# Attention weights and output gradients copied from SBUF to SBUF in place of a store and a load through DRAM

## The chip, the cores and the metric

One NeuronCore of a Trainium2 chip runs the whole program. The metric is the device time of one execution in microseconds (us). Before the change the median of three executions was 715.21 us (713.69 to 716.18). TensorE multiplies matrices, VectorE and ScalarE do the elementwise work, GpSimd (POOL in the profile) and SyncE (SP) issue most transfers (304 and 234 of the 567 issues in the trace of the kernel before). The order of each engine's instructions comes with the build: the two profiles of one program (bwd_only and bwd_only_again) have the rows of SyncE and GpSimd in the same order from 450 to 490 us.

## The reference, cut to what matters

```python
h  = x + attention(layernorm(x), wqkv, wo)     # 2048 tokens, D = 512, 32 heads of 16
h2 = h + ffn(layernorm(h), w1, b1, w2, b2)     # 512 -> 1792 -> 512, GELU
# attention: each token sees 8 tokens at distances 0, 2, ..., 14
logits = einsum("bhsd,bhswd->bhsw", q, kg) * scale
attn   = softmax(logits)
o      = einsum("bhsw,bhswd->bhsd", attn, vg)
# outputs: h2, and the gradients of x, wqkv, wo, w1, b1, w2, b2 for a given grad_out
```

## The kernel before

The sequence is worked in four chunks of 512 tokens, forward and then backward. The window of 8 tokens is turned into dense products: VectorE multiplies q by shifted k (`dots`) or weights by shifted v (`wsum`), and TensorE sums the products with a matrix of zeros and ones. These products need their operands in another arrangement over the partitions than the one in which they arise, and in the kernel before the way there leads through DRAM: `put_q` stores, and `att4`, `row4` or `feat4` load in the new arrangement.

```python
def f_attn(c):                       # softmax weights of chunk c
    ...
    put_q(pq, at_r, c, attn[c][:]...)            # four stores on GpSimd's queue

def f_o(c):                          # weighted sums of v
    a4 = att4(fr, at_r, CJ * c, CJ, f"a4_{c}", "a4", 1, 0)   # four loads on SyncE's queue
    for qd in range(Q4):
        v4 = row4(fr, v_r, qd, ...)              # v, also on SyncE's queue
        wsum(fr, ps, a4, v4, ...)                # VectorE: pbo; TensorE: pso

def across(dst, t_):                 # already there: SBUF to SBUF, four copies on SyncE's queue
    for n in range(Q4):
        sync.dma_start(out=dst[:, TC*n:TC*n+TC, :]..., in_=t_[PR*n:PR*n+PR]...)

def b_go(c):                         # backward: gradient of the attention's output
    ...                              # TensorE: ptc, psgo; ScalarE: go
    put_q(pq, go_r, c, go[:]...)

def b_ga(c):
    v4  = feat4(bm, v_r, ...)                    # bv
    go4 = feat4(bm, go_r, CJ * c, CJ, f"go4_{c}", "q4", 1, ...)
    dots(bm, ga, go4, v4, ...)                   # VectorE: pag; TensorE: ga
```

Three large transfers come into the argument: the load of `w2` (1.8 MB, GpSimd's queue, let go by an exponential of chunk 1), the transpose of `w2` into `w2T` (SyncE's queue, let go by an exponential of chunk 3), and in the backward the load of `h1tm`, 2 MB, on GpSimd's queue. In the backward, VectorE's products for attention's gradient are called `pag`, and TensorE's matmuls that sum them `ga`. TensorE's `psx` and the normalization gradients on VectorE (`jlf`, `luf`, `gh`) belong to the feed-forward's gradient of one chunk, into which the dot products of attention's chunk 0 are woven.

## Time and profile before

| | before |
|---|---|
| time, median | 715.21 us |
| TensorE busy, until 300 us | 230 of 300 us |
| VectorE's waits for the weights in the forward | 11.1 us |
| first feed-forward matmul of chunks 0, 1, 2, 3 | 114.6, 165.4, 213.5, 264.4 us |
| start of the last block of psx (called the block) | 448.75 us |
| from there to the end of the profiled span of 714.5 us | 265.8 us |

Rows in order of time of the kernel before: start, length, engine, line, operation, tiles, and in brackets the idle time just before with what ended it.

```profile
461.71 6.21 PE L719 MATMUL psx<-w1T,gh 128*128 128x512 bf16 x28
...
472.90 0.39 PE L320 MATMUL ga<-pag,sel 128*32 128x512 bf16 x1
```

```profile
465.69 0.55 SPq L282 DMA_DIRECT2D go<-go_r  x1
...
471.52 4.62 DVE L313 TENSOR_TENSOR pag<-go,k_first 128x2048 bf16<-128x2048 bf16 x4
```

The loads for chunk 0 go out at 465.69 us; VectorE does the normalization gradients in the meantime, and starts the products (pag) at 471.52.

### The profile page before, as it was taken

Reading aid. Unit: us, or ns where it says so; the run is one execution under the profiler, and the core shown is the slowest. Engines: PE = TensorE matmul, PEld = TensorE weight load, DVE = VectorE, ACT = ScalarE, POOL = GpSimd, SP = SyncE. Lnnn points to the kernel's source line nnn. Section 1 sums busy time; section 2 is a strip of 40 time slices with the busy share of each in tenths; the row PEclk is TensorE's granted clock in tenths of the full one; section 3 lists DMA queues with packets and bytes.
Section 4 is the critical chain, followed back from the end, with each engine's and each line's share of the span. In section 5 each row is a group of like instructions: output and inputs, shape, how many; then the busy total and the mean of one; then the engine's idle time right before and its main releaser. Section 6 shows DMA issues by size and latency. Waiting matters only on the chain.

```text
span 714.5 us, 10264 instructions
## 1 busy us (share of the span) xinstructions
PE 623.8 (87%) x3614; PEld 264.9 (37%) x3682; DVE 556.2 (78%) x919; ACT 395.1 (55%) x548; POOL 209.3 (29%) x318
## 2 busy tenths in 40 slices
PE   1898668779698499899999999999999999999995
PEld 0433222234243134444444444443533333334342
DVE  6467958688972949975988788476989999999654
ACT  4654425877957639945867687551222135357453
POOL 4325323534533432442443433313200310001000
PEclk9999887969989789999999999999999999999999
DMA  8598798664889669666774975849899999976642
GB/s 233 148 271 224 196 374 279 225 247 161 265 288 214 218 176 198 189 210 243 213 201 97 220 175 147 263 108 260 302 327 372 323 332 307 332 278 218 172 82 67
DMA packets 103221, 163.57 MB, mean 229 GB/s; under 512 B 60961, under 2 KB 69250, under 8 KB 103170
## 3 DMA queue, kind: packets, MB, share of 16 engines
q1 hardware_dynamic: 73824, 78.40, 40.3%
q0 software_dynamic: 24720, 80.07, 34.7%
q10 hardware_dynamic: 4626, 4.46, 1.9%
q8 instruction: 28, 0.46, 0.3%
q14 instruction: 23, 0.19, 0.1%
HBM read 90.97 MB, written 56.71 MB: 207 GB/s over the span
## 4 chain that ended last, share of the span: by engine, by line
PE 40%; issue 16%; DMA 15%; DVE 13%; POOL 8%; ACT 7%; SPq 1%; POOLq 0%; ACTq 0%; DVEq 0%
PE psy L892 5%; PE psq L370 5%; PE psq L929 5%; PE psw L788 4%; PE pss L336 3%; DMA at_r<-attn 3%; PE psx L719 2%; PE psw L667 2%; DMA go<-go_r 2%; DMA s_d<-s 2%; PE pswo L918 2%; DMA bs<-s_d 2%; DMA v<-v_r 2%; PE ga L320 2%; POOL x_d L526 1%
## 5 line engine op out<-in xcount | busy, mean ns | idle before, releaser
L330 DVE TENSOR_TENSOR pb<-ba,r 128x2048 bf16<-128x2048 bf16 x96 | 111.4, 1220 | 1.4 <-PE pss L336 0.5
L506 PE MATMUL psf<-ln2T,w 128*128 128x512 bf16 x218 | 57.6, 395 | 14.3 <-ACT u L508 13.6
L535 PE MATMUL ps<-w,g 128*128 128x512 bf16 x216 | 55.3, 379 | 0.3
L788 PE MATMUL psw<-h1tm,ln2a 128*128 128x512 bf16 (+1 forms) x249 | 53.4, 353 | 0.5 <-issue 0.3
L667 PE MATMUL psw<-gout,gtm 128*128 128x512 bf16 x202 | 50.4, 379 | 2.4 <-DMA gtm<-g_d 1.1
L719 PE MATMUL psx<-w1T,gh 128*128 128x512 bf16 x211 | 49.8, 379 | 0.3
L330 DVE TENSOR_TENSOR pbo<-a,v 128x2048 bf16<-128x2048 bf16 x32 | 38.2, 1218 | 15.1 <-DMA a<-at_r 11.1
L372 ACT CAST qkv<-psq 128x512 bf16<-128x512 f32 x48 | 27.6, 585 | 32.1 <-PE psq L370 25.1
L697 PE MATMUL psg<-goutT,w2T 128*128 128x512 bf16 x161 | 41.1, 379 | 0.4
L508 ACT ACTIVATE u<-psf,b1c 128x512 bf16<-128x512 f32 x56 | 35.9, 681 | 9.7 <-PE psf L506 5.0
L506 PEld LDWEIGHTS <-w 128*128 128x128 bf16 x224 | 21.0, 100 | 43.0 <-issue 25.6
L518 ACT ACTIVATE s<-z 128x1024 bf16<-128x1024 bf16 x28 | 29.6, 1060 | 11.7 <-DVE z L516 7.1
L313 DVE TENSOR_TENSOR pag<-go,bv 128x2048 bf16<-128x2048 bf16 x24 | 28.6, 1219 | 9.4 <-DMA go<-go_r 5.7
L710 POOL DMA_DIRECT2D h1tm_d<-th x27 | 20.6, 762 | 52.1 <-ACT th L708 38.5
L863 ACT ACTIVATE gt<-pss 128x512 bf16<-128x512 f32 x32 | 19.1, 597 | 29.0 <-PE pss L336 29.0
L788 PEld LDWEIGHTS <-ln2a 128*128 128x128 bf16 x256 | 22.6, 98 | 29.2 <-issue 11.7
L708 ACT COPY th<-pth 128x1024 bf16<-128x1024 bf16 x27 | 27.0, 999 | 11.6 <-PE pth L706 11.6
L689 ACT ACTIVATE by<-bu 128x1024 bf16<-128x1024 bf16 x21 | 22.2, 1056 | 18.6 <-DVE gb1p L699 16.5
L892 PE MATMUL psy<-wqkvT,gT 128*128 128x512 bf16 x121 | 31.3, 383 | 0.5 <-issue 0.2
L929 PE MATMUL psq<-gt,ln1a 128*128 128x512 bf16 x123 | 31.1, 380 | 0.3 <-issue 0.2
L526 POOL DMA_DIRECT2D g_d<-g x28 | 20.6, 734 | 36.8 <-DVE g L520 34.0
L336 PE MATMUL pss<-pb,sel 128*32 128x512 bf16 x384 | 29.5, 384 | 1.1 <-DVE pb L330 0.6
(221 smaller groups left out, 1361.2 us busy)
## 6 DMA issues: line engine op xcount, KB each, us to landing
v<-v_r SPq DMA_DIRECT2D x16, 576.0 KB, 6.8
r<-go_r SPq DMA_DIRECT2D x16, 576.0 KB, 8.0
r<-k_r SPq DMA_DIRECT2D x16, 576.0 KB, 6.3
r<-q_r SPq DMA_DIRECT2D x16, 576.0 KB, 5.4
g_d<-g POOLq DMA_DIRECT2D x28, 256.0 KB, 4.8
h1tm_d<-th POOLq DMA_DIRECT2D x27, 256.0 KB, 4.4
h1tm<-h1tm_d POOLq DMA_DIRECT2D x3, 2048.0 KB, 12.1
x_d<-u POOLq DMA_DIRECT2D x21, 256.0 KB, 5.1
```

The lines of the kernel that those rows point to most:

```text
L330: last = nc.vector.tensor_tensor(out=pr[:], in0=_ap(a_ap, [a_ap.ap[0], [2 * H, CJ], [0, Q4], [1, H]], off=wh * H + (4 * H * wh if sg else 0)),
L336: mm = nc.tensor.matmul(ps[PR * n:PR * n + PR, :], lhsT=sel4[:], rhs=prs[wh][:, TC * n:TC * n + TC, :, :].rearrange("p j d h -> p (j d h)" ...
L370: nc.tensor.matmul(ps[:], lhsT=ln1T[:, dc, j * P:(j + 1) * P], rhs=wqkv[:, dc, sel * D:(sel + 1) * D], start=(dc == 0), stop=(dc == DC - 1))
L506: nc.tensor.matmul(ps[:], lhsT=w1[0][:, dc, ft * P:(ft + 1) * P], rhs=ln2T[:, dc, :], start=(dc == 0), stop=(dc == DC - 1))
L508: nc.scalar.activation(out=u[:, i, :], in_=ps[:], func=ACT.Identity, bias=b1c[:, ft:ft + 1], scale=1.0)
L535: nc.tensor.matmul(ps[:], lhsT=gs[ft // 2][:, ft % 2, j * P:(j + 1) * P], rhs=w2[0][:, ft, :], start=(ft == 0), stop=False)
L667: nc.tensor.matmul(ps[:], lhsT=gtm[:, t, :], rhs=gout[t // TC][:, t % TC, :], start=(t == 0), stop=(t == NT - 1))
L697: nc.tensor.matmul(ps[:], lhsT=w2T[:, dc, ft * P:(ft + 1) * P], rhs=gT[:, dc, :], start=(dc == 0), stop=(dc == DC - 1))
L719: nc.tensor.matmul(ps[:], lhsT=t1s[ft // 2][:, ft % 2, j * P:(j + 1) * P], rhs=w1T[:, ft, :], start=(ft == 0), stop=(ft == FT - 1))
L788: nc.tensor.matmul(ps[:, 0:nf * P], lhsT=ln2a[:, t // TC, t % TC, dc * P:(dc + 1) * P], rhs=tmx[:, t, 0:nf * P], start=(t == 0), stop=(t = ...
L892: nc.tensor.matmul(ps[:], lhsT=gT[sel][:, g, j * P:(j + 1) * P], rhs=wqkvT[:, sel * G + g, :], start=(n == 0), stop=(n == NJ - 1))
L929: nc.tensor.matmul(ps[:], lhsT=ln1a[t // TC][:, t % TC, dc * P:(dc + 1) * P], rhs=gts[sel, t // TC][:, t % TC, :], start=(t == 0), stop=(t ...
```

## The change

The intent is to replace two hops (store to DRAM, load from DRAM) by one copy within SBUF wherever the consumer waits for it: for the weights in all four chunks of the forward, for the output gradients in chunks 0 and 1 of the backward. In the forward VectorE first turns the four quarters of the weights round (eight copies of 128x512 in all), because the partitions that receive them want them in reverse order. The stores to DRAM stay, since the backward's sums read them.

```diff
 def f_attn(c):
+            if i == 0:
+                back = fr.tile([P, Q4, TC, 2 * H], BF16, name=f"back{c}", tag="e", bufs=2)
+            o_ap, i_ap = back[:, 0, 2 * i, :], attn[c][:, 0, 2 * i, :]
+            st = 2 * H * TC
+            nc.vector.tensor_copy(out=_ap(o_ap, [o_ap.ap[0], [st, Q4], [1, 4 * H]]),
+                                  in_=_ap(i_ap, [i_ap.ap[0], [-st, Q4], [1, 4 * H]], off=(Q4 - 1) * st))
+        a4s[c] = fr.tile([P, CJ, 2 * H], BF16, name=f"a4_{c}", tag="a4", bufs=1)
+        across(a4s[c], back)
         put_q(pq, at_r, c, attn[c][:].rearrange("p s j m -> p s (j m)"))
 def f_o(c):
-        a4 = att4(fr, at_r, CJ * c, CJ, f"a4_{c}", "a4", 1, 0)
+        a4 = a4s.pop(c)
 def b_go(c):
+        if c < 2:
+            go4s[c] = bm.tile([P, CJ, P], BF16, name=f"go4_{c}", tag="q4", bufs=1)
+            across(go4s[c], go)
         put_q(pq, go_r, c, go[:].rearrange("p s j m -> p s (j m)"))
 def b_ga(c):
-        go4 = feat4(bm, go_r, CJ * c, CJ, f"go4_{c}", "q4", 1, ga_key.get(c))
+        go4 = go4s.pop(c) if c in go4s else feat4(bm, go_r, ...)        # cut
```

(The definitions of the dictionaries `a4s` and `go4s` are left out.)

More of the change, by code (lines that the diff above doesn't have):

```diff
@@ L344 @@
     oTs, hs, l2T = {}, {}, {}
-    lT, k4s, q4s = {}, {}, {}
+    lT, k4s, q4s, a4s = {}, {}, {}, {}
     def f_ln1(c):
@@ L737 @@
     ln2a = bm.tile([P, NC, TC, D], BF16, name="ln2a")
+    go4s = {}
     def b_go(c):
@@ L755, in b_ga @@
         v4 = feat4(bm, v_r, PAD + CJ * c - HALO, CJ + HALO, f"bv4_{c}", "k4", 1, ga_key.get(c))
-        go4 = feat4(bm, go_r, CJ * c, CJ, f"go4_{c}", "q4", 1, ga_key.get(c))
+        go4 = go4s.pop(c) if c in go4s else feat4(bm, go_r, CJ * c, CJ, f"go4_{c}", "q4", 1, ga_key.get(c))
         gl = get(bm, [P, Q4, TC, 2 * H], BF16, f"gl{c}", "gl", 1)
```

## The prediction

> **What bounds the kernel now.** I read the busy table first, then the stretches of 20 us, then the waits of the groups that the change touches, and last the order of time round each of these waits.
>
> ```profile
> PE 623.8 (87%) x3614; PEld 264.9 (37%) x3682; DVE 556.2 (78%) x919; ACT 395.1 (55%) x548; POOL 209.3 (29%) x318
> ...
> PE 40%; issue 16%; DMA 15%; DVE 13%; POOL 8%; ACT 7%; SPq 1%; POOLq 0%; ACTq 0%; DVEq 0%
> ...
> L330 DVE TENSOR_TENSOR pbo<-a,v 128x2048 bf16<-128x2048 bf16 x32 | 38.2, 1218 | 15.1 <-DMA a<-at_r 11.1
> L313 DVE TENSOR_TENSOR pag<-go,bv 128x2048 bf16<-128x2048 bf16 x24 | 28.6, 1219 | 9.4 <-DMA go<-go_r 5.7
> ```
>
> TensorE is the bound, but not evenly. Over the stretches of 20 us, its busy time up to 300 us sums to 230.3 us, so about 70 us are idle there; from 300 to 660 us it is idle for only 11 us in all. So a wait removed in the forward can be worth its full length, while the backward has almost nothing to give until the tail. The two waits named in these rows (11.1 and 5.7 us of DVE idle) are what the change aims at. VectorE has its own dense part: from 580 to 660 us it is 99% busy (79.03 of 80 us) beside a TensorE that is 98% busy (78.11).
>
> The wait of 11.1 us is two events, in chunks 1 and 3; chunks 0 and 2 find their weights already there. The rows are VectorE's, then TensorE's just after:
>
> ```profile
> 104.46 1.22 DVE L330 TENSOR_TENSOR pbo<-a,v 128x2048 bf16<-128x2048 bf16 x1 [3.33 <-DMA a<-at_r]
> ...
> 231.77 1.23 DVE L330 TENSOR_TENSOR pbo<-a,v 128x2048 bf16<-128x2048 bf16 x1 [7.73 <-DMA a<-at_r]
> ```
>
> ```profile
> 106.94 0.97 PE L336 MATMUL pso<-pbo,sel 128*32 128x512 bf16 x8 [3.75 <-DVE pbo L330]
> ...
> 237.39 2.29 PE L506 MATMUL psf<-ln2T,w 128*128 128x512 bf16 x5 [6.88 <-ACT u L508]
> ```
>
> The second is seen in stretches too: TensorE has half a microsecond of work in five, and then runs at half its clock.
>
> ```profile
> 225.00:230.00 5.00, 4.32 (x21) 1.83 (x19) 0.00 (x0) 2.56 (x4) 1.45 (x2) 1.00 1.03 300
> 230.00:235.00 5.00, 0.51 (x3) 0.11 (x2) 3.23 (x5) 0.24 (x1) 1.10 (x2) 0.84 0.11 38
> 235.00:240.00 5.00, 2.39 (x6) 0.94 (x7) 4.48 (x8) 3.83 (x5) 1.59 (x3) 0.50 0.51 170
> ```
>
> Why it is so long is in the chain of waits and in SyncE's queue: the store of the weights takes 11.80 us to land, while the transpose of w2 (18.3 us from issue to landing) fills the DMA engines; only then are the loads issued.
>
> ```profile
> 214.02 11.80 DMA at_r<-attn
> ...
> 210.09 10.04 SPq L602 DMA_TRANSPOSE w2T<-in_B_w_dram  x1
> 227.10 2.40 SPq L300 DMA_DIRECT2D a<-at_r  x4
> ```
>
> [...] at_r<-attn lands in 3.8 us (median) and a<-at_r in 5.8, while the SBUF to SBUF copies that the kernel already has land in 4.6 (early<-qkv) and 3.3 us (k_first<-qkv). One hop of about 4 us replaces two of about 10. [...] here a tensor_scalar of 128x1024 takes 0.42 us, a tensor_tensor of that size 0.69.
>
> **The change part by part.** Added on VectorE: 8 copies of 128x512 bf16, which turn the four quarters round. The nearest row is the normalization's tensor_scalar of 128x512, 1.38 us for four, so 0.3 to 0.35 each, some 2.6 us in all. In chunks 0, 1 and 3 they fall into gaps (VectorE waits 2.73 us at 69.67, 4.67 at 95.80, 7.73 at 231.77); in chunk 2 VectorE is 92% busy, so 0.6 us may be on the path. On SyncE's queue: four issues of 64 KB for four, equal; in the backward four of 128 KB in place of one load, some 2 us of issue instead of 0.55, twice. The stores to DRAM stay, as the backward reads them, but nobody waits for them soon. Some 2 MB of HBM reads out of 90.97 become copies within SBUF.
>
> Chunk 1: the weights are done at 85.4 us, but the buffer for them is single, and VectorE reads chunk 0's until 91.1. So the copies are issued at about 91.5 rather than 93.97, and faster (2.4 against 4.57 us), and land at about 98; the v loads behind them leave some 4 us earlier. VectorE reaches this point at 101.1, so the 3.33 us go, and the 0.27 us for v. TensorE's 3.75 us of waiting follow. Worth 3.4 us.
>
> Chunk 2: there is no wait to remove, but the instruction orders of the two kernels differ here: the weighted sums are placed ahead of half of the GELU pieces (z, g), which puts the last sum about 5 us earlier on VectorE. TensorE idles 6.6 us in this stretch (180 to 200 us), so some of that can be had; against it, the second exponential now comes after the first half's weights and their copy. I take 2 us.
>
> Chunk 3: the copies still sit behind the transpose of w2 in SyncE's order. The exponential that gates the transpose moves ahead of two PSUM copies on ScalarE, so the transpose should start and land 4 to 5 us earlier, at about 223; the copies at about 225, 6.5 us before 231.77. But the new order of VectorE puts two sums ahead of the first GELU piece, which in the old order ran during the wait. Until the weights land TensorE then lacks GELU inputs. I count about 3.2 us of VectorE work that used to fit into the wait and 1.5 us of extra stalls on ScalarE: 6.5 - 4.7 = 1.8 us.
>
> Backward: chunk 0's go is complete at 458.9; the copy lands near 463, and the new order has its 8 products before the last three normalization gradients, where VectorE had gaps of 1 to 4 us; before, they began at 471.5. Chunk 1's wait of 2.22 us goes, and the sums of the backward start some 6 us earlier. But TensorE is saturated: between 440 and 520 us it idles 3.45 us, later almost nothing, and the long DMA waits for go in the chain (8.25 and 7.78 us) belong to chunks 2 and 3, which are not changed. The earlier end of the sums can shorten the wait for the transposed gradients in the tail (2.4 us). I take 2 us.
>
> Sum: 3.4 + 2 + 1.8 + 2 = 9.2 us at the places; I let 1.5 us be lost in waits further on (stores of u, s and g have latencies up to 7.4 us in the chain), hence 7.7 us: 715.2 - 7.7 = 707.5 us.
>
> **The rivals.** First, the waits are only renamed in chunk 3: the copies land with the transpose, VectorE blocks at the new, earlier place of the sums, and TensorE starves longer and cold. For: the 10.04 us of issue in SyncE's order and the new order. Against: the transpose can start earlier. It would cost 1 to 3 us there, leaving about 711. Second, the full gain: the copies escape the transpose, both TensorE waits (3.75 and 6.88 us) vanish with the cold clock after them (some 2 us), chunk 2 gives 4 and the tail 3: 16 to 18 us, about 698. For: these are the idle times of the page. [...] Third, the backward part alone is hidden by a saturated TensorE: then it gives 0 to 0.5 us; 709 in total.
>
> **Range and chances.** The first and third rival together give 713, a good half of the second 700; so 8 in 10 lie between 700.5 and 713. Faster by 2% needs less than 700.9: that takes nearly all of the second, 0.11. Slower by 2% would need 14 us of new waits, for which only a longer blocked chunk 3 speaks: 0.02. Within 2%: 0.87.
>
> **What would show it.** Right: no row of a<-at_r, its wait (11.1 us) below 5 us, and in chunk 3 a wait for a<-back of several us that ends near the landing of w2T; TensorE idle before 300 us down from 70 to about 63; TensorE's backward idle nearly the same; the wait for go down from 5.7 to about 3.5, all in chunks 2 and 3; copies of 0.3 us. Wrong: if the wait in chunk 3 vanishes [...], if it grows beyond 7.7 us, or if the backward from 440 us on shortens by more than 4 us.

## More of the kernel before

The page and the waits of the forward stand in the prediction. Of the backward it shows no rows, so here they are: first TensorE alone in two stretches, counted from the start of the block. The columns are the stretch, its length, TensorE's busy time with its instructions, the granted clock, the busy share of the DMA engines and GB/s.

```profile
448.75:528.75 80.00, 77.14 (x472) 1.00 0.79 246
528.75:618.75 90.00, 86.93 (x565) 1.00 0.98 334
```

TensorE is busy for 77.14 of 80 us at full clock.

## The result, and the profile after

The changed kernel took 733.88 us (median of four, 733.07 to 734.38), against 714.45 us of the kernel before in the same rounds. A ratio here is the mean time of one kernel's fast runs over that of the other's fast runs of the same rounds, so not quite the ratio of the medians: 1.0268, with a 95% interval from 1.0243 to 1.0292. It is slower by over 2%, outside the predicted range. In a later session the same kernel gave 1.0171 (1.0126 to 1.0217); both are slower, the second not clearly by 2%, and how much is known only to about a per cent.

First the page's rows of the two groups that the prediction named. They answer to the third and fourth line of the prediction's first fence.

```profile
L330 DVE TENSOR_TENSOR pbo<-a,v 128x2048 bf16<-128x2048 bf16 x32 | 38.2, 1216 | 16.4 <-PE pso L336 8.4
L313 DVE TENSOR_TENSOR pag<-go,bv 128x2048 bf16<-128x2048 bf16 x24 | 28.7, 1219 | 9.8 <-DMA bv<-v_r 5.1
```

Neither idle time went down. The one before the weighted sums rose from 15.1 to 16.4 us, and its largest part is now a wait for TensorE; the wait for the weights themselves fell from 11.1 to 8.0 us, where the prediction wanted less than 5. The one before the dot products rose from 9.4 to 9.8, now mostly for the load of v. This second row holds chunks 1 to 3 alone. Chunk 0's eight products are in another group (pag<-go,k_first, too small for the page), and that one says more: before the change it had 1.3 us of idle time, all for TensorE, so there was no wait for a load to remove; now it has 8.9 us, all for the copies. For the rest one has to go to the place.

**Chunk 1 of the forward.** GpSimd's rows, to be read for their order, first of the kernel before, then of the changed one:

```profile
85.74 2.17 POOL L179 DMA_DIRECT2D at_r<-attn  x4 [10.84 <-DVE attn L440]
87.90 1.13 POOL L587 DMA_DIRECT2D w<-in_B_w_dram  x1
```

```profile
82.47 1.12 POOL L595 DMA_DIRECT2D w<-in_B_w_dram  x1 [2.48 <-DVE pbo L330]
86.89 1.11 POOL L179 DMA_DIRECT2D at_r<-attn  x2 [3.31 <-DVE attn L440]
```

The load of w2 now stands ahead of the stores of chunk 1's weights; before, it was issued behind them. The chain of waits and ScalarE's row show a store that SyncE issued a moment after it:

```profile
84.04 9.47 DMA k_r<-qkv
```

```profile
93.69 0.59 ACT L459 CAST otm<-pso 128x512 bf16<-128x512 f32 x1 [5.65 <-DMA k_r<-qkv]
```

The store of the keys takes 9.47 us to land, and ScalarE, whose next output reuses that buffer, waits 5.65 us for it (that the load of w2 is behind this, an experiment below shows). The feed-forward of chunk 0, which follows, starts at 119.0 us rather than 114.6.

**Chunk 3 of the forward.** VectorE's row and the same three stretches that the prediction shows of before (columns as there: busy time of TensorE, of its weight loads, of VectorE, ScalarE and GpSimd, then clock and DMA):

```profile
228.11 2.36 DVE L330 TENSOR_TENSOR pbo<-a,v 128x2048 bf16<-128x2048 bf16 x2 [7.53 <-DMA a<-back]
```

```profile
225.00:230.00 5.00, 5.00 (x23) 2.06 (x22) 1.89 (x2) 3.78 (x5) 0.72 (x1) 1.00 0.71 263
230.00:235.00 5.00, 1.32 (x7) 0.49 (x5) 4.97 (x9) 2.41 (x3) 0.72 (x2) 0.95 0.00 0
235.00:240.00 5.00, 4.67 (x15) 1.71 (x15) 2.17 (x5) 4.49 (x6) 3.55 (x5) 0.71 0.81 272
```

The wait for the copies is as long as that for the loads was (7.53 and 7.73 us), as predicted; the copies are issued from 219.67 us, right behind the transpose, whose issue held SyncE for 8.71 us, and VectorE goes on 6.40 us after the last issue. But the wait ends 3.7 us earlier, and the stretch after it is filled again (4.67 of 5 us at a granted clock of 0.71, before 2.39 at 0.50).

**The backward.** From the start of the block, at 451.67 us here, TensorE's two stretches are these:

```profile
451.67:531.67 80.00, 70.90 (x406) 0.96 0.72 196
531.67:621.67 90.00, 85.15 (x537) 0.98 0.92 322
```

Against 77.14 us, 6.2 us of work are missing in the first 80 us, and part of the rest ran at a lower clock (0.51 from 470 to 472 us). From the block's start to the end the changed kernel takes 280.6 us in place of 265.8. So of the 17.8 us by which the profiled spans differ, 14.9 lie here and 2.9 before. The rows at the place, TensorE first, then VectorE and SyncE:

```profile
464.63 0.38 PE L727 MATMUL psx<-w1T,gh 128*128 128x512 bf16 x1
469.32 0.38 PE L320 MATMUL ga<-pag,sel 128*32 128x512 bf16 x1 [4.31 <-DVE pag L313]
469.63 1.51 PE L727 MATMUL psx<-w1T,gh 128*128 128x512 bf16 x4
...
497.06 0.38 PE L320 MATMUL ga<-pag,sel 128*32 128x512 bf16 x1 [4.60 <-DVE pag L313]
```

```profile
468.05 2.36 DVE L313 TENSOR_TENSOR pag<-go,k_first 128x2048 bf16<-128x2048 bf16 x2 [8.03 <-DMA go<-go]
...
495.78 1.23 DVE L313 TENSOR_TENSOR pag<-go,bv 128x2048 bf16<-128x2048 bf16 x1 [5.08 <-DMA bv<-v_r]
```

```profile
461.56 3.58 SPq L384 DMA_DIRECT2D go<-go  x4
...
483.97 3.83 SPq L384 DMA_DIRECT2D go<-go  x4
487.84 1.80 SPq L282 DMA_DIRECT2D bv<-v_r  x1
```

The copies of chunk 0 bring the products forward by only 3.5 us (468.05 for 471.52; 6.4 us when both are counted from the start of the block). But in the new order the first ga stands in the middle of psx: TensorE has begun a sum of 14 psx (the one at 464.63 us is its first), does not go on with it, and waits 4.31 us; the other 13 psx of that sum all come after this ga in its rows. The next four psx take 1.51 us, some 0.38 each, where 28 took 6.21 us before, 0.22 each: the granted clock was 0.64 over these four, and 1.00 over the 28. In chunk 1 the load of v stands behind the copies in SyncE's queue, and TensorE waits 4.60 us for its products.

### The profile page after: what moved, and what is told of

Same layout as the page of the kernel before. It is cut to its first block, busy times and chain, and to the rows that moved or that the text cites. A ratio compares the mean times of both kernels' runs of the same rounds, so it can differ in the third digit from the quotient of the medians.

```text
span 732.3 us, 10337 instructions
## 1 busy us (share of the span) xinstructions
PE 636.7 (87%) x3682; PEld 266.8 (36%) x3682; DVE 556.6 (76%) x927; ACT 396.2 (54%) x548; POOL 211.6 (29%) x318
## 4 chain that ended last, share of the span: by engine, by line
PE 44%; DVE 18%; DMA 12%; issue 10%; ACT 9%; POOL 5%; SPq 2%; POOLq 0%; ACTq 0%; DVEq 0%
PE psq L370 5%; PE psy L905 5%; PE psq L942 5%; PE psw L801 4%; PE psx L727 3%; PE psw L675 3%; PE pss L336 3%; DVE pb L330 2%; DMA gl_r<-gl 2%; PE psf L514 2%; DVE pa L313 2%; PE psgo L756 2%; ACT bu L486 2%; PE ga L320 2%; DVE gh L707 1%
## 5 line engine op out<-in xcount | busy, mean ns | idle before, releaser
L675 PE MATMUL psw<-gout,gtm 128*128 128x512 bf16 x208 | 52.0, 386 | 0.8 <-ACT ow L678 0.7
L727 PE MATMUL psx<-w1T,gh 128*128 128x512 bf16 x216 | 52.4, 387 | 0.0
L330 DVE TENSOR_TENSOR pbo<-a,v 128x2048 bf16<-128x2048 bf16 x32 | 38.2, 1216 | 16.4 <-PE pso L336 8.4
L718 POOL DMA_DIRECT2D h1tm_d<-th x27 | 20.7, 765 | 52.1 <-ACT th L716 37.5
L697 ACT ACTIVATE by<-bu 128x1024 bf16<-128x1024 bf16 x21 | 22.2, 1057 | 19.2 <-DVE gb1p L707 16.4
L727 PEld LDWEIGHTS <-gh 128*128 128x128 bf16 x216 | 20.7, 99 | 29.1 <-issue 7.0
```

The costliest lines, as they stand in the source:

```text
L330: last = nc.vector.tensor_tensor(out=pr[:], in0=_ap(a_ap, [a_ap.ap[0], [2 * H, CJ], [0, Q4], [1, H]], off=wh * H + (4 * H * wh if sg else 0)),
L675: nc.tensor.matmul(ps[:], lhsT=gtm[:, t, :], rhs=gout[t // TC][:, t % TC, :], start=(t == 0), stop=(t == NT - 1))
L727: nc.tensor.matmul(ps[:], lhsT=t1s[ft // 2][:, ft % 2, j * P:(j + 1) * P], rhs=w1T[:, ft, :], start=(ft == 0), stop=(ft == FT - 1))
```

## The experiments

Two tools are used throughout. The order of each engine's instructions can be compared between two builds row by row, before anything runs. And for the backward, I take from each profile the time R from the start of the block to the end of the span, and TensorE's work in the first 80 and the following 90 us, as busy time multiplied by the granted clock (an estimate, from the profile's own columns; the clock is printed to 0.01).

### The two halves alone

```diff
 # fwd_only: the changed kernel, backward as before
-        if c < 2:
+        if c < 0:
             go4s[c] = bm.tile(...)
 # bwd_only: the kernel before with the changes of b_go and b_ga alone
```

> Only the forward part of the change; the backward loads its output gradients from DRAM as before. Theory A (the backward part causes most of the loss, the forward nets about +3 us as the two traces show at 320 to 459 us): about 717.5 us, 716 to 720. Rival B (the forward part starts a delay that grows in the backward): 725 us or more.

> Only the backward part of the change; the forward reaches its weights through DRAM as before. Theory A: about 729 us, 726 to 732, with the first sums of the backward 10 to 16 us later than before. Rival B: within 3 us of the kernel before, 712 to 717.

Measured: the forward part alone 715.51 us, ratio 1.0001 (0.9948 to 1.0053); the backward part alone 727.79 us, ratio 1.0171 (1.0116 to 1.0225). Theory A holds: the loss is the backward's. Its number for the forward was 2 us too high, and the reason is scatter in one profile (see the table under w2). The first of the backward's sums of bwd_only starts at 528.5 us rather than 515.8, 12.7 us later, as expected. The instruction orders confirm that the halves are independent: the changed kernel's order is that of fwd_only until the block, row for row, and that of bwd_only after it.

> The changed kernel once more, to have it beside the others on one chip. If the parts add up (forward 0.0%, backward 1.7%), the ratio is 1.015 to 1.020; if they make each other worse, 1.025 or more again.

Measured: 728.29 us, 1.0171 (1.0126 to 1.0217). The parts add up. This was run because the first measurement, 1.0268, is more than the sum; the two intervals of the same kernel do not overlap, so an interval here covers the scatter within a session, not that between sessions (the sessions of the experiments ran on different chips). R separates better than the times do: in eight profiles of kernels with the backward order of before it lies between 264.5 and 267.5 us (mean 265.4), in four with the changed one (the changed kernel and bwd_only, each twice) between 276.6 and 281.8 (mean 279.4). One of the eight, b_free's below, is slow; without it the mean is the same.

### Is it the copies, or the order around them?

```diff
 # bwd_old: bwd_only, and the dot products of chunk 0 come after the last normalization gradient
+            if nm == "g0_0" and n == 0:
+                gate(first_d, ("rd",))      # first product waits for the last jlf
 ...
-            b_ga(0)
         for n, _ in enumerate(b1_gx(i)):
             take(gw2, 1 if n == 1 else 0)
+        if i == NC - 1:
+            b_ga(0)
 # b_order: the kernel before, with loads
+        if nm == f"f{2 * TC + 1}":
+            gate(rd, ("d", "g0_0", 3))      # second jlf waits for four products
```

> The backward part alone, but the first dot product of chunk 0 is made to come after the last normalization gradient of the pass before it. The instruction orders are then nearly those of the kernel before (876 of 878 rows of VectorE and 7294 of 7366 of TensorE in the same order), with the copies in place of the loads. Theory A (the order costs, not the copies): 712 to 718 us, 10 to 13 us under the backward part alone (727.8). Rival B (the copies, or the load of v behind the copies of chunk 1, cost by themselves): 722 us or more.

> The kernel before, loads and all, but the second normalization gradient of chunk 2 is made to wait for the first four products of chunk 0, which puts VectorE in the order of the changed kernel at this place. Theory A (the order costs): 724 us or more, as the products can begin only at 471.5 us, later than with copies. Rival B (the copies cost): within 3 us of the kernel before.

Measured: bwd_old 718.24 us, ratio 1.0023 (0.9955 to 1.0091), R 266.8 us. No loss is seen of the copies in the old order, and no gain either. TensorE's rows of bwd_old:

```profile
461.92 6.21 PE L721 MATMUL psx<-w1T,gh 128*128 128x512 bf16 x28
...
471.30 0.38 PE L322 MATMUL ga<-pag,sel 128*32 128x512 bf16 x1 [0.24 <-DVE pag L313]
```

But b_order took 716.68 us, ratio 1.0022 (0.9951 to 1.0092), R 263.1 us. VectorE, in the order of the changed kernel at this place, waited longer than in any other of these runs, and no loss is seen. So theory A, as I had written it (VectorE's order costs), is wrong. VectorE's and TensorE's rows of b_order:

```profile
467.76 4.63 DVE L313 TENSOR_TENSOR pag<-go,k_first 128x2048 bf16<-128x2048 bf16 x4 [12.75 <-DMA go<-go_r]
```

```profile
469.25 1.24 PE L670 MATMUL psw<-gout,gtm 128*128 128x512 bf16 x5
470.43 0.39 PE L321 MATMUL ga<-pag,sel 128*32 128x512 bf16 x1
```

In this build TensorE got other matmuls (transposes, psgo of chunk 1, psw) ahead of ga, and ga comes without a wait. An idle VectorE is free here (12.75 us at a ratio of 1.0022), where TensorE has something in its queue before the thing that VectorE owes it. So rival B (the copies cost by themselves) fails in bwd_old and theory A in b_order: the loss is seen only where the copies and the new order come together. TensorE's new order with the loads was never built (see b_pe below).

### One chunk at a time

```diff
-        if c < 2:
+        if c in (0,):          # bwd_c0; (1,) in bwd_c1
```

> The copies in chunk 0 of the backward alone; chunk 1 loads from DRAM. Theory A (the wrong place of chunk 0's products is the larger part, the queue of chunk 1 the smaller): 721 to 726 us. Rival B (it is chunk 1, whose v waits behind its own copies in the queue): 717 or less.

> The copies in chunk 1 of the backward alone. The order up to the first products stays that of the kernel before. Theory A: 714 to 719 us. Rival B (chunk 1's copies and the load of v behind them): 722 or more.

Measured: chunk 0 alone 726.96 us, ratio 1.0147 (1.0093 to 1.0201), with a median a little over the expected range; chunk 1 alone 718.56 us, 1.0022 (0.9960 to 1.0083). By the times chunk 0 is nearly all of it. By R both have a share: 273.3 and 271.6 us against 265.4, so 7.9 and 6.2 us, which add up to 14.1, and the changed order has 14.0. The interval of chunk 1's ratio reaches to 1.0083, some 6 us, so the times don't exclude that share, but they don't show it either.

### SyncE's queue

```diff
-            across(go4s[c], go)
+            across(go4s[c], go, nc.scalar)      # bwd_act: the same copies from ScalarE's queue
```

> The backward part alone, with its copies issued from ScalarE's queue, so that the load of v for chunk 1 no longer stands behind them in SyncE's queue. The order at chunk 0 stays the bad one. Theory (chunk 0's place costs about 8 us, chunk 1's queue about 3): TensorE's wait of 4.2 us at chunk 0 stays, that of 4.1 us at chunk 1 shrinks to 2 or less, total ratio 1.008 to 1.015. Rival (SyncE's queue holds up both): both waits go, ratio under 1.005.

Measured: 728.39 us, ratio 1.0175 (1.0132 to 1.0219), R 279.9 us. Both named waits behaved as the theory said (4.40 us at chunk 0; at chunk 1 only 0.79 us for the products), but the total did not: a wait of 2.85 us for a transposed gradient (gtm) came in at chunk 1, and ScalarE now pays for the issue:

```profile
458.94 4.64 ACTq L384 DMA_DIRECT2D go<-go  x4
463.63 0.60 ACT L646 ACTIVATE luf<-psx 128x512 f32<-128x512 f32 x1 [4.71 <-DMA go<-go]
```

The four issues hold ScalarE for 4.64 us, and the activation that the normalization gradient needs stands behind them. No saving is seen: the issue moved from SyncE (4.22 and 4.11 us in the two profiles of the backward part alone) to ScalarE, with 4.64 us, and the normalization gradient waits for it there.

### The forward: the load of w2

```diff
-    w2.append(fb.tile([P, FT, D], BF16, name="w2", tag="w2", bufs=1))
-    gate(pq.dma_start(out=w2[0][:], ...), ("e", 1, 0))
     ...
     f_o(1)
+    w2.append(fb.tile([P, FT, D], BF16, name="w2", tag="w2", bufs=1))
+    gate(pq.dma_start(out=w2[0][:], ...), ("o", 1, 0))
     f_h(1)
 # fwd_w2late: with the forward copies; b_w2late: in the kernel before
```

> The forward part alone, with the load of w2 emitted after the weighted sums of chunk 1 and gated behind the first of them. Theory (the load of w2, moved ahead of chunk 1's stores by the new order, delays the keys and output rows of chunk 1 and costs about 4.6 us there): feed-forward of chunk 1 starts no later than in the kernel before, total 709 to 713, 5 to 8 us under the forward part alone. Rival (the rows land late for another reason): within 2 us of the forward part alone.

> The kernel before with only the load of w2 emitted and gated later, in the same way. Theory (there the load comes after the stores already and is in nobody's way): within 1.5 us of the kernel before, 713 to 716. Rival (the load of w2 is a cost in both kernels, so that the gain of moving it has nothing to do with the change): 708 to 711.

> The forward part alone with the load of w2 late, once more with more rounds, as its interval reached over 1. Theory: ratio 0.992 to 0.996. Rival (chance): 0.998 to 1.002.

Measured: fwd_w2late 711.40 us, ratio 0.9941 (0.9869 to 1.0013), and once more 714.37 us, 0.9976 (0.9936 to 1.0017); b_w2late 713.96 us, 0.9986 (0.9927 to 1.0045). The times point the expected way and settle nothing: every interval holds 1. The places are clearer, because many profiles share an order. The table gives the start of the first feed-forward matmul of each chunk (mean, and range where there are three profiles or more).

| forward order | profiles | chunk 0 | chunk 1 | chunk 2 | chunk 3 |
|---|---|---|---|---|---|
| before | 11 | 115.1 (112.5 to 116.5) | 166.4 | 214.8 | 264.4 (262.6 to 268.3) |
| changed | 3 | 117.6 (115.6 to 119.0) | 168.8 | 219.9 | 265.5 (263.9 to 267.9) |
| changed, w2 late | 2 | 113.8 | 165.3 | 216.6 | 260.6 |
| before, w2 late | 1 | 113.7 | 165.9 | 213.6 | 262.1 |

The weighted sums of chunk 1 lie before the first column, those of chunk 2 between the second and the third, those of chunk 3 between the third and the fourth. The changed order loses 2.4 us up to the first column, where the ranges still overlap, and another 2.8 us between the second and third (51.2 for 48.4; 50.2 to 52.1 against 48.0 to 49.6), and wins 4.1 us between the third and the fourth (45.5 for 49.6; 41.9 to 47.5 against 48.1 to 51.0): chunks 1, 2 and 3. Holding w2 back takes 3.8 us off the first column (112.2 and 115.4, against 115.6 to 119.0), and SyncE's next load behind the stored keys goes out at 87.2 and 87.5 us rather than at 91.4 to 94.4: the load of w2 is the cause of that delay. No gain is seen over the kernel before with the same move (113.8 and 113.7), and why is open. In the second profile of fwd_w2late VectorE waits for the copies:

```profile
105.59 1.23 DVE L330 TENSOR_TENSOR pbo<-a,v 128x2048 bf16<-128x2048 bf16 x1 [3.40 <-DMA a<-back]
```

That is as long as the wait for the loads was that it was to remove (3.33 us). In the first profile of the same program, however, VectorE starts on the copies at 102.38 us without a wait; they took 3.4 us to land there (median of the four) and 9.1 us in the second.

### The forward: the transpose of w2

```diff
-    gate(sync.dma_start_transpose(out=w2T[:], in_=B_w2[:, :]), ("e", 3, 1))
     mix(f_ffn1(2), f_ffn2(1))
     f_o(3)
+    gate(sync.dma_start_transpose(...), ("o", 3, 0))   # fwd_bothlate: here
     f_h(3)
+    gate(sync.dma_start_transpose(...), ("o", 3, 0))   # fwd_free and b_free: here instead
 # all three with w2 late as well
```

> The same, with the transpose of w2 also emitted later and gated behind the first weighted sum of chunk 3, so that chunk 3's copies no longer stand behind it in SyncE's queue; its result is needed only in the backward. Theory [...]: VectorE's wait for the copies of chunk 3 falls under 1 us and the total is 4 to 7 us under the kernel without this, ratio 0.984 to 0.990. Rival (TensorE is bound there by GELU's inputs anyway): within 2 us of the kernel without.

> The forward part alone, with the load of w2 after chunk 1's sums and the transpose of w2 after chunk 3's residual rows in the queue. Theory (queue order held back both): 3 to 6 us under the kernel with only the first of the two, ratio 0.988 to 0.994. Rival (something else becomes the bound, such as the copies' own 5 us of landing): 0.995 to 1.000.

> The same two moves in the kernel before, weights through DRAM. Theory (copies and moves help each other, as the copies then leave at once): 0.996 to 1.000, so that fwd_free is at least 3 us faster. Rival (the moves are all of it): within 1.5 us of fwd_free.

Measured: fwd_bothlate 722.08 us, ratio 1.0096 (1.0052 to 1.0141); fwd_free 735.71 us, 1.0235 (1.0180 to 1.0291; one of its six runs was slow and is not in the ratio). Both theories are wrong, and in the direction that neither had. b_free gave no verdict: five of its six runs, and the profile, fell in the slow state (median 727.83 us, from 708.52 to 737.90). SyncE's rows of fwd_bothlate, and the waits (what waited, for what: us in all, times, longest) of VectorE there and of TensorE in fwd_free:

```profile
236.30 16.93 SPq L612 DMA_TRANSPOSE w2T<-in_B_w_dram  x1
253.29 1.96 SPq L172 DMA_DIRECT2D xr<-in_A_x_dram  x4
```

```profile
DVE h L472 <- DMA xr<-in_A_x_dram: 7.3, 1, 7.3
```

```profile
PE psw L675 <- DMA gtm_first<-g_d: 21.7, 1, 21.7
```

The copies of chunk 3 got away sooner (214.0 us), and VectorE's wait for them fell only to 2.86 us, as the first product starts 4.9 us after their first issue. But the transpose holds SyncE here too, for 16.93 us, longer than in its old place (10.04). Behind it now wait the residual rows, for which VectorE waits 7.3 us; moved once more, it holds SyncE for 27.98 us and pushes the transposes of w1 and of the first gradient, and TensorE waits 21.7 us. Neither other place was better than the old one, and the prediction's second rival, the full gain, is excluded in this form.

### TensorE's place, and the arrival of the copies

```diff
 # b_pe: the kernel before; a matmul of psx waits for the first ga
+                if (c, j, ft) == (2, 2, 1):
+                    gate(mm, ("ga", "g0_0", 0, 0))
 # bwd_pe: bwd_only, b_ga(0) after the loop as in bwd_old; the first ga waits for the last psx
+                            if (nm, d, n_) == ("g0_0", 0, 0):
+                                gate(mm, ("px",))
```

> The kernel before, with its loads through DRAM; only the third normalization's second matmul of chunk 2 is made to wait for the first matmul of chunk 0's dot products, so that TensorE's order is as bad there as in the changed kernel. Theory A (TensorE's fixed order ahead of late products is the cost, whichever way the gradients come): TensorE waits 7 to 11 us before that matmul, ratio 1.012 to 1.025. Rival B (the copies themselves are needed for the loss): under 1.005.

> The backward part with its copies, VectorE free to take the products early, but the first matmul of chunk 0's dot products held behind the last matmul of the pass before it. Theory A: TensorE's wait of 4.3 us at chunk 0 is gone, ratio 0.998 to 1.006. Rival B (the copies cost by their transfers or queue): 1.012 or more, as the backward part alone.

Measured: b_pe 719.02 us, ratio 1.0053 (1.0005 to 1.0101), R 270.4; bwd_pe 729.56 us, 1.0205 (1.0158 to 1.0251), R 278.6. So theory A failed again, on both sides. In b_pe the dependency was kept, but the build put transposes, psgo of chunk 1 and psw in front of ga, so the first ga came at 470.25 us without a wait; the intended order was not made, and the run tests less than I meant. In bwd_pe ga no longer blocks psx, and TensorE waits all the same:

```profile
469.13 6.04 PE L721 MATMUL psx<-w1T,gh 128*128 128x512 bf16 x14 [4.49 <-DVE luf L655]
```

```profile
464.18 1.23 DVE L313 TENSOR_TENSOR pag<-go,k_first 128x2048 bf16<-128x2048 bf16 x1 [8.01 <-DMA go<-go]
```

VectorE waits 8.01 us for the copies, in order, and the normalization gradient behind that wait (luf) is what frees the accumulator for the next psx. A second path with the same length. My reading of what is common to all slow versions is therefore not one engine's order but that TensorE, directly or through VectorE, has the copies in front of it and too little else in its queue. If so, copies that land sooner must help with all orders left alone:

```diff
-            load_tmx(2, 4)                 # h1tm, 2 MB, GpSimd's queue
             mix(b_go(0), none)
             b_ga(0)
+            load_tmx(2, 4)                 # bwd_tm: gated behind the first product of chunk 0
```

> The backward part alone once more: ratio 1.014 to 1.021, TensorE's wait before chunk 0's dot products 4 to 4.5 us, copies of chunk 0 landing 6 to 7 us after their issue.

> As bwd_only_again, with one 2 MB load moved behind the first product of chunk 0 and all other orders the same. Theory (late arrival in a fixed order): the copies of chunk 0 land in 4 us or less, TensorE's wait before them falls from 4.3 to 0.5 to 2 us and its half clock after it goes, the total is 3 to 6 us under bwd_only_again, ratio 1.008 to 1.013. Rival (the wait is the order's alone, whatever the copies do): the wait stays at 4 us and the ratio within 0.3% of bwd_only_again.

The build of bwd_tm has the rows of TensorE, VectorE, ScalarE and SyncE in exactly the order of bwd_only_again; one row of GpSimd's is elsewhere. Measured at the place, TensorE's row of bwd_only_again, then its rows of bwd_tm:

```profile
464.64 0.58 PE L320 MATMUL ga<-pag,sel 128*32 128x512 bf16 x1 [4.34 <-DVE pag L313]
```

```profile
462.82 0.38 PE L321 MATMUL ga<-pag,sel 128*32 128x512 bf16 x1 [0.82 <-DVE pag L313]
463.13 1.04 PE L720 MATMUL psx<-w1T,gh 128*128 128x512 bf16 x4
465.84 0.59 PE L321 MATMUL ga<-pag,sel 128*32 128x512 bf16 x1 [1.67 <-DVE pag L313]
466.36 2.31 PE L720 MATMUL psx<-w1T,gh 128*128 128x512 bf16 x5
```

The wait of 4.34 us became 0.82 and 1.67 us, and the psx between them run at full speed (1.04 us for four, as in b_pe). The five psx after the second wait do not: they take 2.31 us, where five took 1.25 us in b_pe, at a granted clock of 0.50 (466.67 to 468.67 us). So the wait shrank, and the half clock that was expected to go stayed. VectorE gets its first product 3.0 us after the first issue rather than 6.5 us (458.56 to 461.55, against 456.85 to 463.36). The last quarters gained less: the 2 MB load now goes out at 463.07, among them, and VectorE's third product starts only at 465.94. R fell from 281.8 to 275.8 us, the latter just under the range of the four. The times, however, do not show it: 728.71 us, ratio 1.0195 (1.0152 to 1.0238), against 730.79 us, 1.0212 (1.0166 to 1.0258) of bwd_only_again. So it is shown, in one profile each, that the competing load is a cause of the wait at chunk 0, with the order held fixed. It is not shown that removing it is worth more than a fraction of a per cent: the expected ratio of 1.008 to 1.013 was missed, and the wait at chunk 1 (3.80 us) stays.

### The account of the backward

One table gathers these profiles. "Missing" is TensorE's work (busy times clock, both stretches, 170 us) against the mean of the eight profiles with the old order, 77.0 + 87.9 = 164.9 us; "longer" is R less their mean of 265.4 us.

| kernel | missing, us | longer, us | ratio of times |
|---|---|---|---|
| changed order, mean of four | 13.9 | 14.0 | 1.017 to 1.027 |
| bwd_act | 15.2 | 14.5 | 1.0175 |
| bwd_pe | 13.7 | 13.2 | 1.0205 |
| bwd_tm | 9.4 | 10.4 | 1.0195 |
| bwd_c0 | 7.4 | 7.9 | 1.0147 |
| b_pe | 4.7 | 5.0 | 1.0053 |
| bwd_c1 | 3.3 | 6.2 | 1.0022 |
| bwd_old | -0.2 | 1.4 | 1.0023 |
| b_order | -1.9 | -2.3 | 1.0022 |

For example, the changed order has on average 70.8 us busy at clock 0.943 and 85.1 us at 0.99, which is 66.8 + 84.2 = 151.0. Except for bwd_c1 the two columns agree within 1.7 us (single profiles of the first row up to 3.4): the delay is, within that, work that TensorE did not do in the 170 us after the start of the block, three quarters of it in the first 80. What is lost there is not caught up later; the old order has 164.9 us of work in these 170, so little room is left.

The same estimate in slices of 10 us says where. Of the 17 slices three hold 11.5 us of a loss that comes to 12.9 in this finer count:

| TensorE's work, us, in the slice after the start of the block | 10 to 20 | 40 to 50 | 140 to 150 |
|---|---|---|---|
| old order, mean of eight | 10.0 | 8.1 | 9.9 |
| changed order, mean of four | 4.9 | 4.5 | 7.2 |
| bwd_c0 | 5.0 | 8.4 | 9.0 |
| bwd_c1 | 10.0 | 6.3 | 9.7 |
| bwd_tm | 6.4 | 6.4 | 6.6 |

The first slice holds the wait at chunk 0 with the low clock after it, the second that at chunk 1 (bwd_c1 loses another 1.9 us in the slice after). Each chunk alone loses in its own slice and not in the other's, so chunk 1's share is there at the place. The third, 2.7 us, lies in the backward's sums: waits of TensorE for VectorE's products (pss, 2.1 to 3.3 us in all in the four profiles, 0.6 in the kernel before) and one of 1.2 us for a copy on ScalarE; no experiment took it apart. And bwd_tm won only 1.9 us in the first slice over bwd_only_again (4.5), which fits a time that hardly moved.

## Why the prediction was wrong

The range (700.5 to 713 us) missed 733.88 us. Step by step:

**Backward, "I take 2 us": the step that failed.** The prediction had the copy of chunk 0 landing near 463 us and its products filling gaps of VectorE "where VectorE had gaps of 1 to 4 us". They started at 468.05, which is 465.1 on the clock of the kernel before, as the block starts 2.9 us later; the first copy took 6.46 us to land, beside the 2 MB load, and the four 5.8 to 8.4, where "One hop of about 4 us" was reckoned. And it took TensorE's saturation as a reason why nothing much could happen ("TensorE is saturated", so little to gain). The runs showed that here, on the saturated engine, a late operand cost its full wait (4.31 us at chunk 0), and more where the clock dropped (to 0.51 from 470 to 472 us): 14.0 us of R in place of a gain of 2, and the sums that were to start some 6 us earlier start 15.7 us later (531.5 for 515.8). The third rival came nearest ("hidden by a saturated TensorE: then it gives 0 to 0.5 us"), and bwd_old, with the order as it was, bears it out (1.0023, no gain seen); that the new order could itself lose was nobody's rival. The prediction had seen the new order ("the new order has its 8 products before the last three normalization gradients") and read it as a promise of earlier work. Beside the order it should have asked what TensorE has in its queue before the first ga, and found a single psx. It is shown that the copies in the new order cost and the copies in the old one are not seen to, and that the waits at the two chunks hold most of the 14.0 us; the rest, in the sums, stays open.

**"Chunk 1's wait of 2.22 us goes."** It was replaced: the load of v stood behind the copies, 5.08 us of wait for VectorE and 4.60 for TensorE.

**Chunk 1 of the forward, worth 3.4 us: wrong.** Three profiles against eleven show a loss of 2.4 us, with overlapping ranges, and no gain. The prediction followed the copies and not the load of w2, which the new order let out first. The copies that were to be issued at about 91.5 us went out at 99.06, in SyncE's queue behind a load (94.06) that stood behind the stored keys. With w2 held back they went out at 93.00 and 93.62; "One hop of about 4 us" then held in one profile (3.4 us) and not in the other (9.1), and no gain over the kernel before with the same move is seen.

**Chunk 2, "I take 2 us": wrong**, a loss of 2.8 us between the two feed-forward starts. No experiment took this apart; its cause is open.

**Chunk 3, 1.8 us: wait right, size low.** That the copies would land only after the transpose was an estimate. They stood behind the transpose in SyncE's queue (8.71 us of issue), the wait stayed (7.53 us) and ended earlier; what held them after their own issue was not shown; the step is 4.1 us shorter. By the clock the transpose started no earlier (210.85 for 210.09 us), but counted from the feed-forward of chunk 2 it did, by 6.2 us. The first rival (waits renamed at a cost) is thereby refuted in chunk 3, while it describes chunk 1 well. The second (the full gain) was tried with the transpose elsewhere, and each other place tried cost more than it gave.

**Copies on VectorE**: 0.28 to 0.30 us each, expected 0.30 to 0.35. Right.

**Chances.** "Slower by 2% would need 14 us of new waits, for which only a longer blocked chunk 3 speaks: 0.02." It did need 14 us, and they came from the stretch that the prediction had declared inert. None of the versions tried is shown to beat the kernel before; the nearest, the forward copies with w2 late, gave 0.9941 and 0.9976, with intervals that hold 1.

## What to carry to other kernels

When a change shortens a path to one operand, do not ask only which wait it removes: lay the new instruction order beside the old one and ask, at the first consumer on the busiest engine, what that engine has in its queue before it and whether the operand can be there by then under the traffic of that moment. In this kernel the saturated engine (77.14 of 80 us busy) had little to gain and much to lose (14.0 us of R), while an idle one could wait without cost (VectorE's 12.75 us in b_order). Split the change, count the work that the bound engine did not do in a fixed stretch, and believe a gain at a place only when the end moves too.

## What the runs measured of transfers, clock and waits

- Small copies within SBUF beside a large transfer: four of 128 KB took 5.8 to 8.4 us each at chunk 0 of the changed kernel, with a 2 MB load under way; VectorE had its first product 6.5 us after the first issue with that load (bwd_only_again) and 3.0 us after it without (bwd_tm).
- Issue: one of these copies took 0.77 us of issue and 6.9 to landing (medians at the same place), but four in a row held ScalarE's queue for 4.64 us and SyncE's for 2.49 to 4.22 us, and the activation behind ScalarE's four waited 4.71 us.
- A large transpose from DRAM under traffic: the issue of w2T held SyncE's queue for 10.04 us in its old place in the kernel before, 8.71 us there in the changed one, and 16.93 us and 27.98 us in the two later places.
- Clock: an idle time of 4.31 us was followed by matmuls of 0.38 us in place of 0.22 (granted clock 0.64), so the wait cost more than its length (4.7 us of work in its slice of 10 us).
- Waits: 12.75 us of VectorE's waiting came with no loss that is seen (ratio 1.0022), while TensorE's waits of 4.31 and 4.60 us in the same stretch came with a backward longer by 14 us.
